# Unequal first tiles (384, 192, 448, then 512 tokens) in a fused sliding-window attention and gated feed-forward kernel

## The chip, the core and the metric

The kernel runs on one core of a Trainium2 chip. TensorE (PE in the profile, PEld for its weight loads) multiplies, VectorE (DVE), ScalarE (ACT) and GpSimd (POOL) do the rest, and the DMA queues of SyncE (SP) and POOL move data between HBM and the on-chip memory SBUF. TensorE writes its sums to PSUM, which has eight banks of 128 partitions x 512 fp32 numbers. The metric is the device time of one execution in microseconds.

## The reference

```
scores = q @ k^T / 8                      # batch 8, heads 8, 576 positions, 64 columns a head
attn   = softmax over the last 64 positions, the own one included
x      = (attn @ v), heads joined         # 4608 tokens x 512
gate   = max(x @ w_gate, 0)               # 512 x 1536
val    = x @ w_val                        # 512 x 1536
out    = (gate * val) @ w_out             # 1536 x 512, result 4608 x 512 in fp32
```

All three weights and q, k, v come in fp32; the kernel computes in fp16 with fp32 sums.

## The kernel before, in words

**Tiles.** The 4608 tokens are taken in tiles: four of 384 tokens (numbers 0 to 3) and six of 512 (4 to 9). For each tile there is an attention part, which makes `xt` (x, transposed, in fp16), a hidden part (gate and val, multiplied into `g_sb`) and an output part (`g_sb` times `wo`).

**Two ways to multiply.** The hidden part of tiles 0 and 1 is done plainly (`first_hidden` for the first four of the 12 blocks of 128 hidden columns, then `hidden`; matmuls at L638, L643 and L605). From tile 2 on, `fast_hidden` (L709) uses seven block products in place of eight: P1 to P7, on sums of quarters of the weights (`us`, `vs`, made by `w_form`, L539) and of x (`xc`, made by `x_form`, L517). The quarters of a weight are columns 0 to 767 against 768 to 1535, so a weight sum needs both halves of a weight. Snapshots of running sums go from PSUM to `pr` (ACT, L728), to another bank (`seed`, ACT, L718), are added by DVE (L745) and multiplied by DVE or POOL (L734). Outputs are plain for tiles 0 and 1 (`output`, L1100) and 2 and 3 (`fast_output`, L842), and by seven products for tiles 4 to 9 (`SevenOut`, `SevenLast`, L922), which need sums of `wo` (`o_form`, L863, on POOL).

**Attention.** The scores of tiles 0 to 3 are made in units of 192 tokens (`u_st`, `u_exp`, `u_mask`, `u_pv`, `u_norm`, `u_turn`), those of the later tiles in quads of four windows of 64 tokens (`q_st`, `q_exp` L441, `q_mask` L446, `values`: `t_pv` L476, `t_recip`, `t_norm` L495, `t_turn` L501). A batch of 576 positions is loaded by POOL's DMA queue (`qk_load`, `v_load`); q and k are then transposed by DVE (L199), and rows of v are copied to a second place (`v_spread`: by SP's DMA at L217 or by an engine's copy at L215).

**Order.** No scheduler runs: the program is issued in an order that a small planner, `Weaver`, sets. PE's work is written down in order and advances a clock; work for other engines is put into a heap with a time (`W.at(T, fn)`) and issued when that clock has passed T, or earlier when something is needed. In the output part of tile 3, three rows of 128 tokens, `values` of tile 4 come ahead of the first two rows and `scores` of tile 5's two quads ahead of the last two; tile 4's own quads were scored in the output part of tile 2. On each engine the instructions then run strictly in the order of issue. PSUM banks are handed out by `one_bank`/`two_banks` in turn for tiles 0 and 1, and by a list of free banks (`bank`) later; a matmul that starts a bank waits until the engine that read its last content is done. `behind_masks`, `behind_quad` put a tiny POOL copy into POOL's queue that waits for a mask on DVE, so that POOL's next long operation starts only after it.

**In time.** PE begins the hidden part of tile 0 at 15.1 us. Weights come in load groups of four blocks (`G3`, `V3`, `O3`), from 7.5 us on. Tiles 0 and 1 with their outputs take until 68.1 us, tile 2 until 92.5 us, tile 3 until 117.3 us, the six tiles of 512 to the end. Within tile 0, PE works on blocks 4 to 7 in banks 0 to 3 (four matmul groups of gate weights, then four of val weights), and then starts blocks 8, 9 and 10 in banks 0, 1 and 2, which DVE's `gate` (L586) has to free; between these, `u_pv(2)` (L347) is done, in banks 4 and 5.

Of the kernel before, what the change touches and what calls it, by code (L numbers as in the profile page):

```python
# [47 lines left out]
def kernel(  # L48
# [24 lines left out]
    NS = 4  # L73
    NL = (NT - NS * TT) // WT
    assert NT == NS * TT + NL * WT and TT % 128 == 0
    starts = [TT * t for t in range(NS)] + [NS * TT + WT * t for t in range(NL)]
    widths = [TT] * NS + [WT] * NL

# [347 lines left out]
    def q_window(qd, i):  # L426
        return NS * TT // 64 + QW * qd + i

    def q_st(qd, banks=None):
# [4 lines left out]
                   for hh in range(2) for i in range(QW)] for g in range(G)])  # L434
        written.update((id(to), 512) for to in d["st"])
        return 0.72

    def q_exp(qd, g, give=True):
        d = quads[qd]
        d["p"][g] = a_p.tile([128, 2 * QW, 64], FP16, name="pw", tag="p")  # L440
        nc.scalar.activation(d["p"][g].rearrange("p n c -> p (n c)"), d["st"][g], ACT.Exp, scale=scale)  # L441
        read(d["st"][g], give)

    def q_mask(qd, g):
        d = quads[qd]
        nc.vector.tensor_tensor(d["p"][g], d["p"][g], mask[:, None, :].to_broadcast([128, 2 * QW, 64]), MUL)  # L446
        d["masked"] = d.get("masked", 0) + 1

    def scores(qd, T, banks=None, give=True):

        W.clock += q_st(qd, banks)
        for g in range(G):
            late = 0.8 if qd > 4 and qd % 2 and g == G - 1 else 0.0
# [3 lines left out]
    def t_pv(t, hh, banks, give):  # L457

        if t not in wides:
            wides[t] = {"pv": {}, "give": give, "x": a_n.tile([128, 2, WS, 2, D // 2], FP16, name="xw", bufs=1),  # L460
# [5 lines left out]
        for qh in range(2):  # L466
            qd = 2 * (t - NS) + qh
            while quads[qd].get("masked", 0) < G:
                W.pop()
            for i in range(QW):  # L470
# [10 lines left out]
    def t_part(d, hh, k):  # L481

        s0, s1 = BS * k, min(BS * k + BS, WS)
        return d["pv"][hh][k][:, 0:(s1 - s0) * VW].rearrange("p (s c) -> p s c", c=VW), s0, s1

    def t_recip(t, hh):
        d = wides[t]
        for k in (2, 0, 1):
# [3 lines left out]
    def t_norm(t, hh, k):  # L492
        d = wides[t]
        pv, s0, s1 = t_part(d, hh, k)
        nc.vector.tensor_tensor(d["x"][:, hh, s0:s1], pv[:, :, 0:D].rearrange("p s (c e) -> p s e c", e=2),  # L495
                                d["r"][:, hh, s0:s1, :, None].to_broadcast([128, s1 - s0, 2, D // 2]), MUL)
        read(d["pv"][hh][k], d["give"])

    def t_turn(t, hh):
        dst = xt_tile(t)[:, 2 * hh:2 * hh + 2].rearrange("p e (s c) -> p s e c", c=32)  # L500
        nc.vector.transpose(dst, wides[t]["x"][:, hh])  # L501
# [9 lines left out]
    def x_form(t, n):  # L511
# [5 lines left out]
        (nc.vector if t <= NS or t - 1 in FAST_OUT else nc.gpsimd).tensor_tensor(xc[:, n], x, y, SUB)  # L517
        if n == 3:
            normed[0] = t

    def values(t, hh, T, banks=None, give=False, turn=2.7):
# [4 lines left out]
        for i, k in enumerate((2, 0, 1)):  # L526
# [5 lines left out]
    def w_form(eng, wt, n, j):  # L532
# [3 lines left out]
        f = slice(256 * j + 128 * HF, 256 * j + 128 * HF + 256)  # L536
        a11, a12, a21, a22 = wt[:, 0:2, c], wt[:, 2:4, c], wt[:, 0:2, f], wt[:, 2:4, f]
# [30 lines left out]
    def hidden(t, spans, f0=0, f1=NF, each=1, halves={}, split=(), banks=None):  # L568

        if t not in gs:  # L570
            gs[t] = g_sb_p.tile([128, NF, WT], FP16, name="g_sb"), {}
        g_sb, done = gs[t]
# [12 lines left out]
        def gate(f, c0, r_sb, h2):  # L585
            nc.vector.tensor_tensor(g_sb[:, f:f + w, c0:c0 + n], part(r_sb), part(h2), MUL)  # L586
            done.update(dict.fromkeys(range(f, f + w), c0 + n))

        for fb in range(f0, f1, each):
            r2s = [f_sb.tile([128, 2, WT], FP32, name="pr", bufs=4) for _ in range(2)]  # L590
            r_sbs = {}
            for i, wt in enumerate((wg, wv)):
                items = [(c0, f) for c0, _ in spans for f in range(fb, fb + each, w)]
                first = halves.get((fb, i), 1)
                for group in [items[:first]] + [[item] for item in items[first:]]:
                    hs = [singles[banks.pop(0)] if banks else one_bank() for _ in group]
                    part_written(hs)
                    for cs in ((0, 1), (2, 3)) if len(group) > 1 else (range(NC),):
                        for (c0, f), h in zip(group, hs):
                            for b in range(w):  # L600
                                W.advance(W.clock)
                                w_need(wt, f + b, cs[-1] // 2)
                                m = n // 2 if i == 0 and f in split else n
# [67 lines left out]
    def fast_hidden(t, seven=None):  # L671

        g_sb, done = gs[t] = g_sb_p.tile([128, NF, WT], FP16, name="g_sb"), {}
# [4 lines left out]
        gh = g_sb[:, :, 0:TW].rearrange("p f (h n) -> p f h n", h=2)  # L678
# [4 lines left out]
        def operands(name, wt, sums, j):  # L683
            c = slice(256 * j, 256 * j + 256)
            f = slice(256 * j + 128 * HF, 256 * j + 128 * HF + 256)
            return {"P1": (wt[:, 0:2, c], b11), "P2": (wt[:, 2:4, c], b21), "P3": (sums[:, 3, :, c], b22),
# [45 lines left out]
        def mult(eng, j, n, h, r, v, to=None):  # L732
            f = 2 * j + HF * n
# [5 lines left out]
        def add(j, name, i, n, delay):  # L739

            def summed():
# [11 lines left out]
                else:  # L753
                    def product_of():
                        late = seven and j == last
                        mult(nc.vector if late else nc.gpsimd, j, n, 1, pr[:, 0], pr[:, 1])
                        if late and n == 1 and t != LAST - 1:
                            nc.gpsimd.tensor_copy(last2[0:1], g_sb[0:1, HF + 2 * j, WT // 2:WT // 2 + 2])
                            g_form(nc.gpsimd, t, 1, j - 1)
                            g_form(nc.gpsimd, t, 2, 0)  # L760
                        if seven and n == 0:
                            for s in range(1 if j == last - 1 and t != LAST - 1 else 2):
                                g_form(nc.vector if late else nc.gpsimd, t, s, j)
                            if late:
                                for jj in (j,) if t + 2 <= LAST else (j, 1) if t == LAST else range(3):
                                    g_form(nc.vector, t, 2, jj)
                                nc.gpsimd.tensor_copy(last2[0:1], g_sb[0:1, HF - 1, 0:2])
# [646 lines left out]
```

## Time and profile before

| what | value |
|---|---|
| median of 3 runs | 300.97 us (300.72 to 301.99) |
| the profiled execution | 300.6 us, of it 298.9 us span |
| granted clock | 0.999 |
| PE busy | 288.8 us, 4657 matmuls recorded |
| DVE, ACT, POOL busy | 251.7, 196.9, 200.8 us |
| from the first full hidden matmuls to tile 4 | 15.6 to 117.3 us |
| tiles 4 to 9 | 117.3 to 298.9 us |

The span is what lies between the first and the last instruction; some 1.7 us of the profiled execution lie around it. A busy PE is not PE at its peak, since matmuls overlap and their ends are modelled: what counts is the distance from one matmul's start to the next one's, which the timeline gives for a run of equal matmuls. A few matmul records are missing, so counts in the views can be a little under those of the program.

### The profile page before, as it was taken

The page shows a single profiled execution, that of the slowest core. Times are in us where ns is not written, and L with a number is a line of the kernel's source. Part 1 is how long each engine was busy: PE and PEld are TensorE (multiplying, and loading weights), DVE is VectorE, ACT ScalarE, POOL GpSimd, SP SyncE. Part 2 cuts the span into 40 slices and gives each one's busy share as a digit, 9 for nine tenths or more (in the row PEclk, how much of TensorE's full clock was granted, in tenths as well). Part 3 has the DMA queues.
Part 4 walks back from the last instruction along what each step waited for, and adds up shares of the span by engine and source line. Part 5 has one row for each costly group of instructions (what it writes and reads, how often), then busy time and mean ns, then how long its engine had stood idle before and what let it go on. Part 6 is the DMA issues. An engine that isn't in the chain of part 4 may idle for free.

```text
span 298.9 us, 11099 instructions
## 1 busy us (share of the span) xinstructions
PE 288.8 (97%) x4657; PEld 239.9 (80%) x4657; DVE 251.7 (84%) x513; ACT 196.9 (66%) x410; POOL 200.8 (67%) x240
## 2 busy tenths in 40 slices
PE   4799999999999999999999999999999999999994
PEld 2486867949958966888888888888888888888894
DVE  5948986998995899779999999989858985896584
ACT  3745236358848847984798579857985798538850
POOL 8768699858967883985958595759375617441750
PEclk9999999999999999999999999999999999999999
DMA  7999999989919636911499239922911210021013
GB/s 215 181 197 201 195 194 185 194 149 191 81 43 201 156 83 129 141 42 36 69 220 119 55 59 219 125 56 58 172 35 36 76 38 0 3 100 45 1 37 105
DMA packets 59506, 33.20 MB, mean 111 GB/s; under 512 B 39552, under 2 KB 53824, under 8 KB 59456
## 3 DMA queue, kind: packets, MB, share of 16 engines
q0 software_dynamic: 46688, 18.29, 52.5%
q1 hardware_dynamic: 12192, 13.75, 15.3%
q8 instruction: 36, 0.59, 0.8%
q10 hardware_dynamic: 576, 0.46, 0.5%
q14 instruction: 14, 0.11, 0.1%
HBM read 37.75 MB, written 9.44 MB: 158 GB/s over the span
## 4 chain that ended last, share of the span: by engine, by line
PE 94%; DVE 3%; DMA 1%; ACT 0%; issue 0%; DVEq 0%
PE bank L709 46%; PE bank L922 18%; PE bank L605 9%; PE bank L842 5%; PE bank L1100 5%; PE bank L276 4%; PE bank L476 3%; PE bank L347 1%; DMA vs<-in_k_dram 1%; PE bank L643 1%; DVE qT L199 1%; DVE kT L199 1%; PE bank L638 0%; PE bank L240 0%; ACT nats L192 0%; DVE pr L1088 0%
## 5 line engine op out<-in xcount | busy, mean ns | idle before, releaser
L734 POOL TENSOR_TENSOR g_sb<-pr 128x512 f16<-128x512 f32 (+1 forms) x36 | 42.7, 1191 | 42.6 <-ACT pr L751 42.5
L745 DVE TENSOR_TENSOR pr<-bank,pr 128x512 f32<-128x512 f32 (+1 forms) x96 | 58.5, 650 | 3.6 <-PE bank L709 1.9
L728 ACT COPY pr<-bank 128x512 f32<-128x512 f32 (+1 forms) x96 | 49.1, 566 | 13.7 <-PE bank L709 13.5
L734 DVE TENSOR_TENSOR g_sb<-r,bank 128x512 f16<-128x512 f32 (+1 forms) x48 | 31.3, 652 | 22.8 <-ACT r L778 22.2
L922 PEld LDWEIGHTS <-g_sb 128*128 128x128 f16 x444 | 41.8, 98 | 5.0
L709 PE MATMUL bank<-xc,us 128*128 128x256 f16 (+2 forms) x292 | 41.3, 265 | 0.0
L709 PE MATMUL bank<-xc,vs 128*128 128x256 f16 (+2 forms) x292 | 41.3, 265 | 0.0
L709 PEld LDWEIGHTS <-vs 128*128 128x128 f16 x388 | 36.6, 98 | 3.4
L709 PEld LDWEIGHTS <-us 128*128 128x128 f16 x388 | 36.6, 98 | 3.2
L205 POOL DMA_DIRECT2D v<-in_v_dram x41 | 34.8, 873 | 2.2 <-DMA nats<-in_q_dram 1.0
L751 ACT ACTIVATE pr<-pr 128x512 f32<-128x512 f32 (+1 forms) x48 | 29.3, 610 | 9.7 <-DVE pr L745 9.7
L778 ACT ACTIVATE r<-bank 128x512 f32<-128x512 f32 (+1 forms) x48 | 27.7, 576 | 4.9 <-PE bank L709 4.0
L709 PEld LDWEIGHTS <-wg 128*128 128x128 f16 x288 | 27.4, 98 | 3.2
L709 PEld LDWEIGHTS <-wv 128*128 128x128 f16 x288 | 27.4, 98 | 2.6
L709 PE MATMUL bank<-xt,wv 128*128 128x256 f16 (+1 forms) x192 | 27.5, 266 | 0.0
L709 PE MATMUL bank<-xt,wg 128*128 128x256 f16 (+1 forms) x192 | 27.5, 266 | 0.0
L872 POOL TENSOR_TENSOR g_sb<-g_sb,xus 128x512 f16<-128x512 f16 x24 | 27.0, 1145 | 0.0
L922 PE MATMUL bank<-wo,g_sb 128*128 128x256 f16 (+1 forms) x222 | 26.6, 270 | 0.0
L441 ACT ACTIVATE pw<-bank 128x512 f16<-128x512 f32 x48 | 25.3, 607 | 1.1 <-PE bank L276 0.7
L922 PE MATMUL bank<-wts,g_sb 128*128 128x256 f16 (+1 forms) x222 | 25.6, 270 | 0.0
L718 ACT COPY bank<-bank 128x512 f32<-128x512 f32 (+1 forms) x48 | 24.5, 552 | 0.0
L310 ACT ACTIVATE p<-bank 128x384 f16<-128x384 f32 (+1 forms) x40 | 14.2, 444 | 10.0 <-PE bank L276 9.9
(120 smaller groups left out, 557.1 us busy)
## 6 DMA issues: line engine op xcount, KB each, us to landing
out_dram<-o_sb SPq DMA_DIRECT2D x30, 256.0 KB, 3.2
nats<-in_k_dram POOLq DMA_DIRECT2D x15, 288.0 KB, 5.5
nats<-in_q_dram POOLq DMA_DIRECT2D x15, 288.0 KB, 8.0
v<-in_v_dram POOLq DMA_DIRECT2D x31, 128.0 KB, 8.0
v<-v SPq DMA_DIRECT2D x27, 66.0 KB, 3.1
v<-v SPq DMA_DIRECT2D x13, 132.0 KB, 2.5
wg<-in_moe_w_gate_dram POOLq DMA_DIRECT2D x6, 256.0 KB, 6.5
wv<-in_moe_w_val_dram POOLq DMA_DIRECT2D x6, 256.0 KB, 8.1
```

The lines of the kernel that those rows point to most:

```text
L205: nc.gpsimd.dma_start(v16s[b % 2][lo:hi, g, :, 0:64], v[b, :, 64 * g - 64 + lo:64 * g - 64 + hi].rearrange("h p d -> p h d"))
L441: nc.scalar.activation(d["p"][g].rearrange("p n c -> p (n c)"), d["st"][g], ACT.Exp, scale=scale)
L605: nc.tensor.matmul(h[:, b * n + lo:b * n + lo + m], wt[:, c, (f + b) * 128:(f + b) * 128 + 128], xt[:, c, c0 + lo:c0 + lo + m], start=(c = ...
L709: nc.tensor.matmul(to[:, HT * m + lo:HT * m + lo + step], w[:, k, 128 * m:128 * m + 128], x[:, k, lo:lo + step], start=(first and m == 0 a ...
L718: nc.scalar.copy(at[j, "B", i][:, 0:TW], at[j, "A", i][:, 0:TW])
L728: nc.scalar.copy(pr[:, i], at[j, "A", i][:, 0:TW])
L734: eng.tensor_tensor(gh[:, f:f + 2, h], pair(r), pair(v), MUL)
L745: nc.vector.tensor_tensor(pr[:, i], to[:, 0:TW], pr[:, i], ADD)
L751: nc.scalar.activation(pr[:, 0], pr[:, 0], ACT.Relu)
L778: nc.scalar.activation(r, to[:, 0:TW], ACT.Relu)
L872: eng.tensor_tensor(to, x, y, op)
L922: nc.tensor.matmul(at[key][:, QN * m * whole:QN * m * whole + n1 - n0], A[:, 128 * m:128 * m + 128], B[:, c, n0:n1], start=(first and m == ...
```

## The change

The tiles become 384, 192, 448 and seven of 512 tokens (numbers 0 to 9 again). Tiles 0 and 1 are plain, so 576 tokens have plain hidden parts instead of 768; tiles 2 to 9 use the seven products in the hidden part. Tile 1's last 64 tokens have their hidden values put in front of tile 2's in `g_sb`, so that outputs are made for 512 tokens (0 and 1 together, minus those 64) and 512 tokens (the 64 and tile 2). The outputs of the first 512 tokens are made in one go, four rows of 128 tokens for each load group of `wo`. Outputs by seven products still begin at tile 4.

The quarters of the weights are now taken within a load group (two blocks of 128 against the next two), so a weight sum needs one load group only. Fourteen of the 24 sums are made by DVE at 16.2, 20.9 and 29.7 us of the planner's clock: four before and eight behind the gates of `first_hidden`, the eight ahead of the masks of unit 2, and two behind unit 2's transposes; ten are POOL's, from 44.7 us on. Before, DVE made eight (at 48.2 and 64.5) and POOL sixteen. Batch 1's tokens all belong to tiles 2 and 3 (quads instead of units), v of that batch is loaded between the load groups of `wo`, and part of it is spread by DVE copies. In the output part of tiles 2 and 3, the scores of the next tile's quads come first and its values one row of output later; tile 5's quads follow, the last after the last row. Some 512-column and 384-column matmuls are issued as two halves (`SPLIT`, `OUT_SPLIT`).

```
-    NS = 4
-    NL = (NT - NS * TT) // WT
-    starts = [TT * t for t in range(NS)] + [NS * TT + WT * t for t in range(NL)]
-    widths = [TT] * NS + [WT] * NL
+    NS = 2
+    NQ = WT - (TT + U) % WT
+    NL = (NT - TT - U - NQ) // WT
+    widths = [TT, U, NQ] + [WT] * NL
+    starts = [sum(widths[:t]) for t in range(len(widths))]
...
+    def q_wins(qd):
+        return range(NQ // 64 - QW if qd == 1 else QW)
...
-            late = 0.8 if qd > 4 and qd % 2 and g == G - 1 else 0.0
+            late = 0.8 if qd > 8 and qd % 2 and g == G - 1 else 0.0
...
+    def behind_x(t):
+        nc.gpsimd.tensor_copy(last[0:1], xc_tile(t)[0:1, 3, 0, 0:2])
...
     def w_form(eng, wt, n, j):
         c = slice(256 * j, 256 * j + 256)
-        f = slice(256 * j + 128 * HF, 256 * j + 128 * HF + 256)
-        a11, a12, a21, a22 = wt[:, 0:2, c], wt[:, 2:4, c], wt[:, 0:2, f], wt[:, 2:4, f]
+        a11, a12, a21, a22 = (wt[:, 2 * k:2 * k + 2, 512 * j + 256 * m:512 * j + 256 * m + 256] for m in range(2) for k in range(2))
...
         def gate(f, c0, r_sb, h2):
-            nc.vector.tensor_tensor(g_sb[:, f:f + w, c0:c0 + n], part(r_sb), part(h2), MUL)
-            done.update(dict.fromkeys(range(f, f + w), c0 + n))
+            if t == 0:
+                nc.vector.tensor_tensor(g_sb[:, f:f + w, c0:c0 + n], part(r_sb), part(h2), MUL)
+                done.update(dict.fromkeys(range(f, f + w), c0 + n))
+                return
+            m = WT - TT
+            nc.vector.tensor_tensor(g_sb[:, f:f + w, TT:WT], part(r_sb)[:, :, 0:m], part(h2)[:, :, 0:m], MUL)
+            nc.vector.tensor_tensor(gs[2][0][:, f:f + w, 0:n - m], part(r_sb)[:, :, m:n], part(h2)[:, :, m:n], MUL)
...
-                                m = n // 2 if i == 0 and f in split else n
+                                m = n // 2 if (i, f) in split else n
...
-    F_LAST = [f for j in range(NF // 4) for f in (2 * j + HF, 2 * j + HF + 1, 2 * j, 2 * j + 1)]
+    F_LAST = [f for j in range(NF // 4) for f in (4 * j + 2, 4 * j + 3, 4 * j, 4 * j + 1)]
...
-        n = DM // 2 if t == 0 and NF - 1 > f >= 9 else DM
+        n = DM // 2 if NF - 1 > f >= OUT_SPLIT else DM
...
+    SPLIT, OUT_SPLIT = [(0, 4 + i) for i in range(8)] + [(1, 4 + i) for i in range(4)], 3
...
-        for n in range(3):
-            w_load(*O3[n], 38.6 + 2.6 * n)
-        for u in (4, 5):
-            v_load(u)
+        w_load(*O3[0], 38.6)
+        v_load(4)
+        v_load(5, ((7, 0, 128),))
+        for n in (1, 2):
+            w_load(*O3[n], 39.6 + 2.6 * n)
+        v_load(5, ((NG - 1, 64, 128),))
...
+        W.at(37.9, lambda: scores(0, 37.9, singles[4:8], False))
+        W.at(41.2, lambda: scores(1, 41.2, singles[4:8], False))
+        W.at(44.6, lambda: behind_quad(1))
+        for hh, T in enumerate((45.0, 45.7)):
+            W.at(T, lambda hh=hh, T=T: values(2, hh, T, singles[4 + 2 * hh:6 + 2 * hh], True, 1.75))
+        for n, T in enumerate((46.8, 49.2, 49.3, 49.4)):
+            W.at(T, lambda n=n: x_form(2, n))
+        W.at(36.4, lambda: v_spread(3, pool))
+        for u in (4, 5):
+            W.at(41.9, lambda u=u: v_spread(u, dve))
+        plan_batch(2, (36.5, 36.6, 38.0, 38.1), (52.9, 53.0, 57.5, 62.0))
+        W.at(50.5, lambda: behind_x(2))
...
-        for T, gap, eng, some in ((41.5, 0.1, nc.gpsimd, sums[0][:4] + sums[1][:3]), (52.8, 0.1, nc.gpsimd, sums[1][3:8]),
-                                  (48.2, 0.6, nc.vector, sums[0][4:8]), (68.1, 0.1, nc.gpsimd, sums[0][8:]),
-                                  (64.5, 0.7, nc.vector, sums[1][8:])):
+        for T, gap, eng, some in ((16.2, 0.0, nc.vector, sums[0][:4]), (20.9, 0.0, nc.vector, sums[1][:4] + sums[0][4:8]),
+                                  (29.7, 0.0, nc.vector, sums[1][4:6]),
+                                  (44.7, 0.1, nc.gpsimd, sums[1][6:8] + sums[0][8:10]), (50.6, 0.1, nc.gpsimd, sums[0][10:12] + sums[1][8:])):
...
-        hidden(0, ((0, TT),), 4, NF, 4, split=(4, 5), halves={(8, 0): 3, (8, 1): 2})
+        hidden(0, ((0, TT),), 4, NF, 4, split=SPLIT, halves={(8, 0): 3, (8, 1): 2})
         hidden(1, ((0, U),), each=4, banks=[0, 1, 4, 5, 2, 3, 0, 1, 2, 3, 0, 1])
         taken["one"] += 2
-        output(0, (0, 1, 2), (0, 4, 8, NF))
-        ready(1)
-        hidden(1, ((U, TT),), each=4)
-        output(1)
+        output(0, (0, 1, 2, 3), (0, 4, 8, NF))
...
-            between = [[] for _ in range(widths[t] // 128)]
-            if t + 1 < NS:
-                for u in (2 * t + 2, 2 * t + 3):
-                    between[0].append(lambda u=u: unit_values(u, W.clock))
-            elif t + 1 <= LAST:
-                for hh in range(2):
-                    between[hh].append(lambda hh=hh: values(t + 1, hh, W.clock))
-            if t + 2 <= LAST:
-                for qh in range(2):
-                    between[qh - 2].append(lambda qh=qh: scores(2 * (t + 2 - NS) + qh, W.clock))
+            qd = 2 * (t + 1 - NS)
+            score = lambda n: lambda: scores(qd + n, W.clock)
+            value = lambda hh: lambda: values(t + 1, hh, W.clock)
+            between = [[score(0)], [score(1)], [value(0), value(1)], []]
+            if t == 3:
+                between[3].append(score(2))
             fast_output(t, between)
+            if t == 3:
+                score(3)()
```

## The prediction

> **What bounds the kernel now.** I read the profile's page first, then the chain that ended last, then the timeline of each engine around the places that the change touches.
>
> ```profile
> PE 94%; DVE 3%; DMA 1%; ACT 0%; issue 0%; DVEq 0%
> ```
>
> TensorE carries 94% of the chain; the rest is the start, ahead of 15.6 us, and the tail. So a shorter matmul stream shortens the run, and everything else counts only where PE has to wait for it. From the chain, in order of time (start, us, what):
>
> ```profile
> 27.42 10.60 PE bank L605 x100
> ...
> 68.11 14.07 PE bank L709 x168
> 82.18 0.96 PE bank L347 x86
> ...
> 92.49 14.12 PE bank L709 x168
> ...
> 147.62 16.59 PE bank L709 x152
> 164.22 1.31 PE bank L922 x12
> ```
>
> 152 matmuls of 256 columns take 16.60 us, 109.2 ns each. The two 384-wide tiles need 14.07 and 14.12 us for 168 of 192 columns. What 192 and 384 columns cost undisturbed is in PE's timeline:
>
> ```profile
> 26.02 0.92 PE L605 MATMUL bank<-xt,wg 128*128 128x384 f16 x4
> 26.86 0.56 PE L347 MATMUL bank<-v,p 128*32 128x65 f16 x48
> 27.36 2.13 PE L605 MATMUL bank<-xt,wg 128*128 128x384 f16 x12
> 29.32 2.76 PE L605 MATMUL bank<-xt,wv 128*128 128x384 f16 x16
> 31.92 1.48 PE L605 MATMUL bank<-xt,wg 128*128 128x192 f16 x16
> 33.24 1.48 PE L605 MATMUL bank<-xt,wv 128*128 128x192 f16 x16
> ```
>
> From start to start, 16 of 384 columns take 2.60 us (162.5 ns each), 16 of 192 take 1.32 us (82.5 ns). The first line is the place to watch: its four should end at 26.67 and PV follows at 26.86, so PE already waits 0.2 us for DVE to free a bank.
>
> **Part 1, the matmul stream.** In program order the change takes 352 matmuls of 192 columns, 40 of 384 and 26 of 512 out and puts 168 of 224 and 220 of 256 in; scores, PV and the seven-product outputs keep their counts. 512 columns cost 225 ns (12 of L842 from 83.08 to 85.78 us); 224 columns are between 82.5 and 109.2, by their middle 95.9 ns. Sum: -352 x 82.5 = -29.04 us, -40 x 162.5 = -6.50, -26 x 225 = -5.85, +168 x 95.9 = +16.11, +220 x 109.2 = +24.02: **-1.26 us**. That is 2304 columns fewer, an eighth of 192 tokens' hidden part, plus what halving the long matmuls gives.
>
> The Trainium skill, page "TensorE: Matmul & The Clock Gate", section "Back-to-back issue gap" (its phase diagram stands just above), puts 512 columns at some 216 ns and 256 at 109 ns. By that, halving a 512 gains nothing, and the sum would be -1.02 us; the rows here say 225 against 2 x 109.2, and the measurement decides.
>
> **Part 2, stalls that go.** 168 x 82.5 is 13.86 us; the two 384-wide tiles lose 0.21 and 0.27 us to ACT's and DVE's work on their products. The 512-wide tiles lose nothing (109.2 each, all through). In their place come a tile of 448, between the two (I leave it 0.1), and one of 512: **-0.38 us**, bounds 0 and -0.48.
>
> **Part 3, eight weight sums on DVE ahead of unit 2's masks.** DVE and POOL before:
>
> ```profile
> 20.41 0.56 DVE L654 TENSOR_TENSOR g_sb<-pr,bank 128x384 f16<-128x384 f32 x1
> 23.40 1.42 DVE L317 TENSOR_TENSOR p<-p,mask 128x384 f16<-128x384 f16 x3 [2.44 <-ACT p L310]
> ...
> 24.75 0.54 DVE L586 TENSOR_TENSOR g_sb<-pr,bank 128x384 f16<-128x384 f32 x1
> 25.21 0.72 DVE L317 TENSOR_TENSOR p<-p,mask 128x384 f16<-128x384 f16 x1
> 25.86 1.47 DVE L586 TENSOR_TENSOR g_sb<-pr,bank 128x384 f16<-128x384 f32 x3
> ```
> ```profile
> 23.83 1.89 POOL L215 COPY v<-v 64x512 f16<-64x512 f16 x2 [2.77 <-DMA v<-in_v_dram]
> ```
>
> DVE is free from 20.9 to 23.4 us, 2.5 us. The eight sums take more: L539 rows of DVE last 0.42 us, follow each other at 0.34, and at 0.45 where one needs the last: 8 sums, 3.2 us, done at 24.1. Their weights are there (the last of them lands at 20.1 us). The masks thus start 0.7 us late, and inside POOL's two copies of v. That matters, as the masks' group shows:
>
> ```profile
> L317 DVE TENSOR_TENSOR p<-p,mask x24: 336/352/1317, 23.4 to 68.3; 128x384 f16<-128x384 f16 x24
> ```
>
> The 1.32 us is the mask at 39.6, which began just behind a POOL sum of 1.15 us and ended after it; the one at 25.21 waited for a copy. DVE's fp16 work in SBUF stands still while POOL runs a tensor operation; gates, which read PSUM, do not (24.75: 0.54). Walked: the first mask waits for copy one (24.6), the second for copy two (25.75), third done at 26.2; gate of bank 0 at 26.7, fourth mask, gate of bank 1 at 27.4. PE wants bank 0 at 26.02 and bank 1 0.33 later: it starts at 26.75, waits again until 27.45, and is at its next matmuls behind PV at 28.29, where it was at 27.36: **+0.93 us**. Bounds: +0.07 if the second mask gets in ahead of copy two (gate of bank 1 at 26.55), +1.6 if a sum is caught by a copy too. I take the walk. Four sums at 16.2 lie in DVE's idle time up to 18.5 and cost nothing; without that, 0.42 each.
>
> The backlog runs on: DVE's queue from 28.35 (reciprocals to transposes 2.2, two sums 0.8, four gates at 0.47, four transposes of q and k at 1.09, two split gates at 0.52) ends near 38.6, and PE wants that bank for quad 0's scores at 38.8. **+0.1**, bounds 0 and +0.6.
>
> **Part 4, transfers and queues.** Two v loads (near 1 us each in the queue) go ahead of the second and third group of `wo`, which then land near 43.8 and 46.4 instead of 41.8 and 44.4. PE uses them at some 45.7 and 50.3: nothing, else 1 us for each us over 1.9. POOL's next issues wait for these landings, so its queue is free at 47.3. Its ten sums of 1.15 us then run, with a wait of 2.5 us for `behind_x`, to 61.5. The tile-2 stage starts near 53.9 and uses the last of them 17 steps of 0.77 us later, at 66: 4 us of cover. DVE's copies of v (1.4 us in all) replace SP transfers and lie ahead of PV at 47.
>
> **Part 5, values one output row after their scores.** Before, PV of tile 4 came a whole hidden part after its masks. Now scores, one row of 12 matmuls (2.70 us), PV: four exps at 0.49, the first 0.2 behind the scores, end at +2.2, the last mask (0.42) at +2.7. No cover is left, and two transposes of 1.09 us are in DVE's queue there. **+0.25 us** in tile 3's output, bounds 0 and +1.5 (one POOL product of 1.28 in the way).
>
> **Part 6, scores behind the last row of tile 3.** Now tile 4 follows on them at once.
>
> ```profile
> 117.31 0.58 ACT L847 COPY o_sb<-bank 128x512 f32<-128x512 f32 x1 [0.62 <-PE bank L842]
> 117.80 1.07 ACT L718 COPY bank<-bank 128x512 f32<-128x512 f32 x2
> ```
>
> In ACT's queue exps and seeds now alternate: exp, seed, exp. With S the start of tile 4's P1: first exp at S+0.2, seed at S+0.69, second exp from S+1.17 to S+1.77. P5's second half starts the bank of that second exp, and PE wants it after P1 (0.87) and 8 short matmuls (0.45), at S+1.32. **+0.45 us**, bounds 0 and +0.6.
>
> **The sum.** -1.26 - 0.38 + 0.93 + 0.1 + 0.25 + 0.45 = **+0.09 us**, on 300.6 of the profiled execution, which is 0.37 under the median of its runs: 301.1 on the median. From 117.3 us on, 181.6 us of matmuls keep their order.
>
> **The rivals.**
> *The masks get through (299.5).* No wait in parts 3 and 5: -1.26 - 0.48 + 0.07 + 0 + 0 + 0.2 = -1.47. For it: DVE is only 0.7 us late and 25.21 shows that a mask can also go between copies; against it, the wait at 26.67 is there already.
> *The lock between DVE and POOL decides (302.9, slower).* Tile 3's output is the place: eight masks stand in front of PV, and POOL works off products of 1.28 us and `wo` sums of 1.15 there. Each mask that starts behind one loses up to its length, as at 39.6; the one collision in my sum costs 0.25 since half a us is spare, each further one its full 1.2. Two more (at both tiles' values) are +2.4, less 0.6 of what part 3 may save: +1.8. It decides from the second further collision on. The Trainium skill, page "SBUF — State Buffer", section "Who interferes with whom", states that a DVE operation with two SBUF inputs and a GpSimd operation that reads SBUF block each other fully; by that rule, the trace agrees (1.32 against 0.35 us).
> *The sums come late (304).* POOL's last ones miss tile 2's third step by more than 4 us, for a queue held by landings. Against it: slack of 4 us. Then tile 2 does not gain what part 1 says, +3.
>
> **How the numbers follow.** 0.5% is 1.5 us, about what a measurement of this kernel can tell from no change. Forecast 0.58 (0.52 of it within 0.5%, 0.02 faster, 0.04 slower), masks through 0.20 (half beyond 0.5%), the lock 0.17 (0.14 slower), late sums 0.05: faster 0.12, same 0.65, slower 0.23. Low ends together: -1.26 - 0.48 + 0.07 = -1.67, 299.3; high: -1.26 + 1.6 + 0.6 + 1.5 + 0.6, less 0.3 for not all at once, = +2.7. I cut both a little: 299.4 to 303.2.
>
> **What would show it.** Right: 152 matmuls of tile 3 at 109 ns, a hole of some 1.1 us in PE between 26 and 28 us with DVE gates as releaser, one of near 0.4 us right behind tile 4's first eight matmuls with ACT as releaser, and tile 4 starting near 116.9 us (117.3 less 0.36). Wrong: no hole near 27 us (then -1), long masks (over 0.5 us) near 105 to 111 us, a PE wait for `us` or `vs` between 62 and 66 us, or any hole in the six last tiles, which I take as unchanged.

## The result and the profile after

The changed kernel takes 301.95 us (median; 301.05 to 302.81), the kernel before 301.01 us (300.49 to 301.99) beside it: ratio 1.0031, 95% interval 1.0021 to 1.0041. Forecast were 301.1 us and "within 0.5%"; that holds, with the median 0.85 us above the forecast. The profiled execution took 301.29 us, of it 299.6 us span (before 298.9). The sum of the prediction is made against profiles, and there it is +0.7 where +0.09 was forecast.

The chain that ended last of the changed kernel, by engine:

```profile
PE 89%; DVE 6%; DMA 1%; issue 1%; ACT 1%; DVEq 0%
```

TensorE still bounds the kernel, but 1% is new: "issue", time in which an engine waited for nothing that the profile shows. Where it is, PE's timeline of the changed kernel says (start, us, line, operation, count; in brackets the idle time before and its releaser):

```profile
26.07 0.49 PE L634 MATMUL bank<-xt,wg 128*128 128x192 f16 x4
26.98 0.49 PE L634 MATMUL bank<-xt,wg 128*128 128x192 f16 x4 [0.42 <-DVE g_sb L609]
27.40 0.56 PE L348 MATMUL bank<-v,p 128*32 128x65 f16 x48
27.89 2.15 PE L634 MATMUL bank<-xt,wg 128*128 128x192 f16 x24
...
117.20 0.61 PE L740 MATMUL bank<-xc,us 128*128 128x128 f16 x8
118.15 0.61 PE L740 MATMUL bank<-xc,vs 128*128 128x128 f16 x8 [0.35 <-ACT pw L450]
...
136.50 1.47 PE L956 MATMUL bank<-wo,g_sb 128*128 128x256 f16 x12
137.90 1.32 PE L493 MATMUL bank<-v,pw 128*32 128x65 f16 x127
139.48 0.19 PE L493 MATMUL bank<-v,pw 128*32 128x65 f16 x1 [0.26 <-issue]
...
198.99 1.34 PE L493 MATMUL bank<-v,pw 128*32 128x65 f16 x128
200.27 0.94 PE L956 MATMUL bank<-wts,xus 128*128 128x256 f16 x7
201.78 0.71 PE L956 MATMUL bank<-wts,xus 128*128 128x256 f16 x5 [0.58 <-issue]
```

The first two groups are the holes that the prediction named, behind DVE's gates and behind ACT's exps. Counted from start to start, beyond the usual distance, they cost 0.58 and 0.51 us. The last two (0.44 and 0.74 us) and a third of 0.28 us at 52.3 us were not foreseen: the trace shows nothing that PE waited for, and it stopped in the middle of a run of equal matmuls. The kernel before has no such hole at these places. Its PE timeline where the last one would be:

```profile
198.85 1.34 PE L476 MATMUL bank<-v,pw 128*32 128x65 f16 x128
200.12 1.48 PE L922 MATMUL bank<-wts,xus 128*128 128x256 f16 x12
```

What ends the hole at 118.15 us is ACT's queue, in which exps (L450) and seeds (L749) alternate as forecast:

```profile
116.43 0.60 ACT L450 ACTIVATE pw<-bank 128x512 f16<-128x512 f32 x1
117.02 0.57 ACT L749 COPY bank<-bank 128x512 f32<-128x512 f32 x1
117.50 0.60 ACT L450 ACTIVATE pw<-bank 128x512 f16<-128x512 f32 x1
117.99 0.61 ACT L749 COPY bank<-bank 128x512 f32<-128x512 f32 x1
```

**Where the time went.** Start to start on PE, before against after. Up to tile 4's first matmul (117.11 against 116.31 us) the change gains 0.80 us; forecast was 0.36. Then tile 4 loses the 0.51, and of the tiles behind it only the spans with holes differ: 30.35 to 31.29 us from tile 4 to 5 (0.51 and 0.44), 30.33 to 30.34, 30.34 to 31.07 (0.74), 30.24 to 30.32 (0.08, one more small hole at 232.4 us). From the last matmul to the end it is 0.30 us shorter; why stays open. -0.80 + 0.51 + 0.44 + 0.01 + 0.73 + 0.08 - 0.30 = +0.67.

### The profile page after: what moved, and what is told of

Same layout as the page of the kernel before. It is cut to its first block, busy times and chain, and to the rows that moved or that the text cites. A ratio compares the mean times of both kernels' runs of the same rounds, so it can differ in the third digit from the quotient of the medians.

```text
span 299.6 us, 10994 instructions
## 1 busy us (share of the span) xinstructions
PE 288.8 (96%) x4627; PEld 242.2 (81%) x4627; DVE 256.7 (86%) x513; ACT 198.7 (66%) x400; POOL 193.9 (65%) x223
## 3 DMA queue, kind: packets, MB, share of 16 engines
q1 hardware_dynamic: 11808, 13.41, 15.1%
## 4 chain that ended last, share of the span: by engine, by line
PE 89%; DVE 6%; DMA 1%; issue 1%; ACT 1%; DVEq 0%
PE bank L740 48%; PE bank L956 19%; PE bank L874 5%; PE bank L634 4%; PE bank L1135 4%; PE bank L493 3%; PE bank L277 3%; DVE kT L200 2%; PE bank L672 1%; DMA vs<-in_k_dram 1%; DVE qT L200 1%; DVE pw L459 1%; PE bank L348 1%; DVE p L318 1%; ACT pw L450 1%
## 5 line engine op out<-in xcount | busy, mean ns | idle before, releaser
L765 POOL TENSOR_TENSOR g_sb<-pr 128x512 f16<-128x512 f32 (+1 forms) x36 | 45.2, 1256 | 41.8 <-ACT pr L782 41.5
L776 DVE TENSOR_TENSOR pr<-bank,pr 128x512 f32<-128x512 f32 (+1 forms) x96 | 60.9, 674 | 3.3 <-PE bank L740 1.9
L759 ACT COPY pr<-bank 128x512 f32<-128x512 f32 (+1 forms) x96 | 51.0, 587 | 14.0 <-PE bank L740 13.9
L765 DVE TENSOR_TENSOR g_sb<-r,bank 128x512 f16<-128x512 f32 (+1 forms) x48 | 32.5, 677 | 22.7 <-ACT r L809 21.0
L740 PE MATMUL bank<-xc,vs 128*128 128x256 f16 (+2 forms) x292 | 42.7, 269 | 0.3 <-ACT pw L450 0.3
L740 PE MATMUL bank<-xc,us 128*128 128x256 f16 (+2 forms) x292 | 42.7, 269 | 0.0
L740 PEld LDWEIGHTS <-vs 128*128 128x128 f16 x388 | 37.6, 98 | 4.3 <-issue 0.5
L450 ACT ACTIVATE pw<-bank 128x512 f16<-128x512 f32 x60 | 32.1, 606 | 2.1 <-PE bank L277 1.7
L749 ACT COPY bank<-bank 128x512 f32<-128x512 f32 (+1 forms) x48 | 25.6, 573 | 0.0
L459 DVE TENSOR_TENSOR pw<-pw,mask 128x512 f16<-128x512 f16 x60 | 23.5, 437 | 2.1 <-ACT pw L450 1.7
```

Source lines behind the costliest of these rows:

```text
L740: nc.tensor.matmul(to[:, HT * m + lo:HT * m + lo + step], w[:, k, 128 * m:128 * m + 128], x[:, k, lo:lo + step], start=(first and m == 0 a ...
L749: nc.scalar.copy(at[j, "B", i][:, 0:TW], at[j, "A", i][:, 0:TW])
L759: nc.scalar.copy(pr[:, i], at[j, "A", i][:, 0:TW])
L765: eng.tensor_tensor(gh[:, f:f + 2, h], pair(r), pair(v), MUL)
L776: nc.vector.tensor_tensor(pr[:, i], to[:, 0:TW], pr[:, i], ADD)
```

## The experiments

Two theories of the holes without a releaser were tested. *Instruction blocks*: PE's instructions come by DMA (queue 8 of the profile: 36 packets, 0.59 MB, so 16 KB each); 9254 weight loads and matmuls over 36 packets are 257 a packet; if a block is 256 instructions, it holds 128 pairs of a weight load and a matmul. A *limit* is the place where one block ends and the next begins. The three holes stand behind pairs 863, 2270 and 3294: 1407 = 11 x 128 - 1 and 1024 = 8 x 128 apart. PV (attention weights times v) of a 512-wide tile is 128 short pairs in 1.35 us, so it can use up a whole block before the next one has come. *Order of work*: some wait of the new order that the trace does not show. The new order itself (parts 3 and 6 of the prediction) was tested beside it.

### 1 and 2: more pairs near 14 us (e1, e2)

In PE's idle time near 14 us, 40 small matmuls of zeros are added (e2: the kernel before, 40 there and 66 in place of a filler):

```
+        for i in range(40):
+            g = 32 * (i % 4)
+            nc.tensor.matmul(to[g:g + 32, 0:16], zero[:, 0:32], zero[:, 0:16], start=False, stop=False, ...)
         heat(1, units[1]["st"][3])
```

> The changed kernel with 40 small matmuls of zeros (32 weights, 16 columns) in TensorE's idle time near 14 us; nothing else moves. Theory of the instruction blocks: TensorE's instructions come in blocks of 16 KB, 256 instructions or 128 pairs of weight load and matmul; the three holes that no engine released (52.3, 139.0 and 200.9 us; 0.28 + 0.44 + 0.74 = 1.46 us) lie 11 and 8 such blocks apart, each where a whole block was a burst of short PV matmuls (128 pairs in 1.4 us), so that the next block was not there yet. 80 more instructions ahead of it move the block limits away from the bursts: no hole without a releaser over 0.15 us, and the time falls by 1.2 to 1.8 us, to 0.994 to 0.998 of the kernel before. Theory of a new wait in the order of work (a semaphore or a transfer that the trace does not show): the holes stay at the same matmuls, and the time stays within 0.3 us of the changed kernel's, 1.002 to 1.004 of before.

> The kernel before with 104 such matmuls net ahead of 14 us (66 in place of one long filler matmul, 40 in the idle time). Theory of the instruction blocks: the limits now fall on the PV bursts of tiles 5 to 8, where the changed kernel has them; by the durations of its own blocks of 128 pairs against 2.45 us (fetch of a block until its first instruction runs), holes without a releaser of 0.5 to 1.1 us at two to four of 139, 170, 200 and 231 us, together 1.5 to 3.3 us, and a time of 1.004 to 1.012 of the kernel before. Theory of a new wait in the order of work: this kernel keeps its order, so no such hole, and 1.000 to 1.002 for the small matmuls themselves.

Measured: 308.41 us (1.0221, interval 1.0176 to 1.0267) and 308.68 us (1.0234, 1.0196 to 1.0271). Both times are missed by far: e1 was to become faster by the first theory and became slower, and e2 became slower by much more than forecast. The holes at 139 and 201 us are gone from e1, and the kernel before, its order untouched, now has them (0.20, 0.25 and 0.80 us, behind or just after the PV of three tiles, and 1.82 us in a burst at 61.4, besides 3.9 us in a PV between the added matmuls). But the added matmuls are themselves a burst of short pairs, at a time when the DMA engines are at least 90% busy (10 to 18 us). PE's timeline of e1:

```profile
14.06 0.35 PE L244 MATMUL bank<-wts 128*32 128x16 f16 x17
17.28 0.32 PE L244 MATMUL bank<-wts 128*32 128x16 f16 x23 [2.86 <-issue]
...
18.42 2.74 PE L673 MATMUL bank<-xt,wg 128*128 128x384 f16 x8
```

PE stops inside the dummies, behind pair 223 = 95 + 128, for 3.0 us. Its block is on the way from 14.90 to 15.79 us, and PE goes on 1.5 us after that. The last line shows a second price: eight matmuls of 384 columns take 320 ns each in place of 162, half speed. The trace's granted clock is 0.5 there (18.4 to 21.8 us), and again from 56.0 to 59.4 us. The shift also brought limits into bursts at 53 and 121 us (2.2 and 1.1 us) and one into long matmuls at 33 us (0.6 us), where the block's packet started 3.7 us behind the limit before it.

### 3 and 4: parts 3 and 6 on top of e1

```
-(20.9, 0.0, nc.vector, sums[1][:4] + sums[0][4:8]),
+(20.9, 0.0, nc.vector, sums[1][:4]), (44.9, 0.0, nc.vector, sums[0][4:8]),      # e3
-                score(3)()
+                scores(qd + 3, W.clock - 0.75)                                   # e4
```

> e1_after_pad40 with four of the eight weight sums of 20.9 us (those of us, second group) on DVE at 44.9 us, behind quad 1's masks. If part 3 of the prediction is right that the eight sums make the masks and gates late: PE's wait at 26.3 us (0.58 us excess) falls to at most 0.2, and the time by 0.4 us against e1; the four sums at 45.7 to 47.4 us are hidden, since DVE is idle there for 1.5 us. If the copies of v on POOL and not the sums hold the masks: the wait stays over 0.4 us, and the time within 0.15 us of e1.

> e1_after_pad40 with the exps of tile 5's second quad planned 0.75 us sooner, so that ACT's queue at the start of tile 4 is copy, exp, exp, seed, exp, seed, exp in place of copy, exp, seed, exp, seed, exp, exp. If part 6 is right that PE waits for the second exp behind a seed: PE's wait at 117.6 us (0.51 us) falls to under 0.1, and the time by 0.4 us against e1. If the seeds are as urgent as the exps: a wait of 0.2 us or more comes back within the next 2 us at the product that follows the seed (P2 or P6), and the time falls by 0.25 or less.

Measured: 308.96 us (1.0245, 1.0209 to 1.0281) and 308.10 us (1.0208, 1.0163 to 1.0254). With holes of 2 to 3 us that come and go the times tell nothing, and e3's wait at DVE's gates was covered by PE's late start. e4's trace does tell. PE's timeline at the start of its tile 4:

```profile
123.97 0.61 PE L746 MATMUL bank<-xc,vs 128*128 128x128 f16 x8
124.42 0.60 PE L746 MATMUL bank<-xc,us 128*128 128x256 f16 x4
125.39 0.60 PE L746 MATMUL bank<-xc,vs 128*128 128x256 f16 x4 [0.37 <-ACT bank L755]
```

P5 no longer waits for the second exp, but P6 waits for the second seed, 0.54 us from start to start: the wait has only moved on. The order that helps must put both exps and both seeds first.

### 5 and 6: the limits moved without a burst (e5, e6)

```
-    HALVED = ((4, 0, 'P5'),)
+    HALVED = ((4, 0, 'P5'),) + tuple((4, 1, p) for p in ('P1', 'P6', 'P2', 'P7', 'P5'))   # e5; e6: 13 products
```

> The changed kernel with five more products of tile 4 in halves of 128 columns (the second step's P1, P6, P2, P7, P5): 40 more pairs of weight load and matmul between 122 and 131 us, no new burst, and nothing earlier moves. Price by 128 columns at 56 ns: 40 x (2 x 56 - 109.2) ns = 0.11 us. Theory of the instruction blocks: from tile 5 on the block limits lie 40 pairs sooner, some 38 matmuls ahead of the PV bursts, as in the kernel before; the holes at 139.0 and 200.9 us go (0.44 + 0.74 us in the profiled execution; by the medians, which lie 0.66 us further apart than the profiles, up to 1.8), the hole at 52.3 us (0.28) stays, and the time is 0.995 to 0.999 of the kernel before. Theory of a wait in the order of work: holes and time as in the changed kernel, 1.003.

> The kernel before with 13 more products of tile 4 in halves of 128 columns: 104 more pairs between 122 and 143 us, price 0.29 us, order of work unchanged. Theory of the instruction blocks: a limit now falls within 10 pairs of the start of the PV bursts of tiles 5 to 8, so a block lasts some 1.6 to 2 us there, and holes without a releaser of 0.2 to 1 us come at two to four of them (139, 170, 200, 231 us), 0.6 to 2.5 us together: 1.003 to 1.009 of the kernel before. Theory of a wait in the changed order of work: no holes, 1.001.

Measured: e5 300.67 us (0.9988, interval 0.9970 to 1.0006), e6 303.32 us (1.0077, 1.0049 to 1.0104). PE's timeline of e5 at the places of the two late holes:

```profile
138.49 1.34 PE L493 MATMUL bank<-v,pw 128*32 128x65 f16 x128
139.77 1.05 PE L956 MATMUL bank<-wts,xus 128*128 128x256 f16 x8
...
199.16 1.34 PE L493 MATMUL bank<-v,pw 128*32 128x65 f16 x128
200.43 1.48 PE L956 MATMUL bank<-wts,xus 128*128 128x256 f16 x12
```

and of e6, the kernel before with more pairs:

```profile
230.88 1.25 PE L476 MATMUL bank<-v,pw 128*32 128x65 f16 x128
232.06 0.72 PE L922 MATMUL bank<-wts,xus 128*128 128x256 f16 x5
233.42 0.92 PE L922 MATMUL bank<-wts,xus 128*128 128x256 f16 x7 [0.64 <-issue]
```

Forty matmuls in halves, which cost 0.11 us by the estimate ahead of the run, make the changed kernel 1.28 us faster by the medians; the intervals against the kernel before do not overlap. The hole at 52.3 us, ahead of the edit, stays (0.26). The other way round, the kernel before with its order unchanged loses 2.25 us, of which halving explains 0.29. Its profile shows one such hole (0.80 us) and a start 1.5 us late, with a granted clock of 0.5 from 11.2 to 14.7 us, so how the rest splits up in the other executions stays open. The clock does not explain the loss: the four executions with a mean clock of 0.998 or more took 302.48 to 303.59 us, and the fastest of them is 1.96 us above the fastest of before. The theory of a wait in the order of work falls.

Over all kernels of this study, 26 holes of 0.2 us and more without a releaser stand behind pair 94 or 95 of a group of 128, counted from PE's first matmul. The only others lie around the long filler matmuls ahead of 14 us, and one of 0.21 us at 58 to 59 us in e1 and e3 is no stop but a matmul at the clock of 0.5.

### 7 and 8: the sums later, and the limit at 52.3 us (e7, e8)

e7 is e5 with e3's edit. e8 adds:

```
-    SPLIT, OUT_SPLIT = [(0, 4 + i) for i in range(8)] + [(1, 4 + i) for i in range(4)], 3
+    SPLIT, OUT_SPLIT = [(0, 4 + i) for i in range(8)], 3
-    HALVED = ... ('P1', 'P6', 'P2', 'P7', 'P5'))
+    HALVED = ... ('P1', 'P6', 'P2', 'P7', 'P5', 'P4', 'P3'))
```

> e5_after_late40 with four of the eight weight sums of 20.9 us on DVE at 44.9 us, behind quad 1's masks. If the eight sums make the masks and gates late (part 3): PE's wait at 26.3 us (0.58 us excess in the changed kernel) falls to at most 0.2 and the time by 0.4 us against e5; the four sums run in DVE's idle time at 45.7 to 47.3 us. If POOL's copies of v hold the masks and not the sums: the wait stays over 0.4 us and the time within 0.15 us of e5.

> e7 with the wv products of the second group of tile 0 not in halves (16 pairs fewer near 24 us, price at 162.5 against 2 x 82.5 ns a gain of 0.04 us) and seven in place of five products of tile 4 in halves (56 pairs more, 0.05 us), so that the limits from tile 5 on are those of e5. Theory of the instruction blocks: the limit at 52.3 us moves 16 pairs on, the block with tile 2's PV bursts (5.1 us long) gets 1.7 us longer, and the hole of 0.28 us goes: 0.3 us less than e7, no hole without a releaser over 0.15 us. If it does not go, something else than the blocks makes that one.

Measured: e7 299.92 us (0.9961, interval 0.9945 to 0.9978), 0.75 us less than e5 in the same series; e8 299.85 us (0.9954, 0.9937 to 0.9971). The eight sums thus do cost time, more than the 0.4 expected: PE's two waits at the gates were 1.05 us in e5's profile, and one of 0.33 us is left in e7's (0.41 in e8's). So neither theory of e7 was whole. In e8 no hole without a releaser over 0.15 us is left behind 15 us, the one at 52.3 us included; its time is only 0.07 us under e7's, less than the two can be told apart by.

The profile of e5 explains the size. DVE's timeline of the changed kernel:

```profile
24.05 1.30 DVE L318 TENSOR_TENSOR p<-p,mask 128x384 f16<-128x384 f16 x3
25.28 0.54 DVE L609 TENSOR_TENSOR g_sb<-pr,bank 128x384 f16<-128x384 f32 x1
```

and of e5, the same program up to tile 4:

```profile
24.11 2.14 DVE L318 TENSOR_TENSOR p<-p,mask 128x384 f16<-128x384 f16 x3
26.18 0.54 DVE L609 TENSOR_TENSOR g_sb<-pr,bank 128x384 f16<-128x384 f32 x1
```

Three masks take 1.30 us in one execution and 2.14 in the other, and the gate behind them, which frees PE's next bank, starts 0.9 us later. In the first POOL's copies of v ran from 24.41 us, in the second, where v landed sooner, from 23.82, over all three masks. PE is at its next matmuls behind PV at 27.89 us in the one and at 28.41 in the other; the prediction's walk said 28.29.

### 9: the copies of v on ACT (e9)

```
-        v_spread(2, pool)
+        nc.gpsimd.tensor_copy(last[0:1], v16s[0][64:65, NG - 1, 0, 0:2])
+        W.at(24.6, lambda: v_spread(2, act))
```

> e8 with unit 2's two copies of v on ACT, behind its four exps, in place of POOL (one tiny POOL copy still waits for the landing of v, so POOL's loads issue when they did). If POOL's copies are what makes unit 2's masks long: each mask takes 0.35 us (three took 2.24 us in e8), PE's wait near 26.5 us (0.41 us) falls to at most 0.1, and the time by 0.3 to 0.4 us against e8. If the masks are held by something else: they stay long and the time stays within 0.15 us.

Measured: 299.21 us (0.9942, interval 0.9929 to 0.9955). DVE's timeline of e8:

```profile
23.46 2.24 DVE L318 TENSOR_TENSOR p<-p,mask 128x384 f16<-128x384 f16 x3 [0.86 <-ACT p L311]
```

and of e9:

```profile
23.30 1.12 DVE L318 TENSOR_TENSOR p<-p,mask 128x384 f16<-128x384 f16 x3 [0.86 <-ACT p L311]
24.34 0.55 DVE L609 TENSOR_TENSOR g_sb<-pr,bank 128x384 f16<-128x384 f32 x1
24.83 0.36 DVE L318 TENSOR_TENSOR p<-p,mask 128x384 f16<-128x384 f16 x1
```

With the copies off POOL the masks take half the time (0.36 us the fourth), the gate runs 1.3 us sooner than in e8, and PE's wait is gone. POOL's copies are shown to be what stretches the masks. The times of e8 and e9 come from two series; by the ratios the gain is 0.36 us, as expected, though the intervals overlap.

### 10: two exps, two seeds (e10)

e8 with the exps of tile 5's second quad at -0.75 us and the last two of them 0.6 us later:

```
-                score(3)()
+                scores(qd + 3, W.clock - 0.75, gap=0.6)
```

> e8 with ACT's queue at the start of tile 4 as copy, exp, exp, seed, seed, exp, exp. e4 moved the wait from the second exp to the second seed (0.54 us at P6 in place of 0.51 at P5), so both orders lack one place. If the chain is only these four: no wait over 0.1 us in tile 4's first 4 us and 0.4 to 0.5 us less than e8. If the last two exps are urgent as well (their banks, or POOL's queue behind quad 7): a wait of 0.3 us or more by 122 us, and less than 0.2 us gained.

Measured: 299.46 us (0.9946, interval 0.9933 to 0.9958). ACT's timeline of e10 at the start of tile 4:

```profile
116.00 1.08 ACT L450 ACTIVATE pw<-bank 128x512 f16<-128x512 f32 x2
116.97 1.09 ACT L750 COPY bank<-bank 128x512 f32<-128x512 f32 x2
117.96 1.11 ACT L450 ACTIVATE pw<-bank 128x512 f16<-128x512 f32 x2
118.93 1.11 ACT L760 COPY pr<-bank 128x512 f32<-128x512 f32 x2
```

P5 and P6 run without a wait. The wait of 0.51 us is gone and one of 0.18 us comes in its place, at 119.6 us behind the snapshots of the last line: 0.33 gained on PE, between the two expectations. By the ratios the time is 0.24 us under e8's, with intervals that overlap.

### 11 and 12: output rows in halves, and all together (e11, e12)

```
-                nc.tensor.matmul(op, g_sb[:, f, ...], wo[:, f], start=(i == 0), stop=(i == NF - 1))
+                n = DM // 2 if (t, sub) in ROWS else DM
+                for lo in range(0, DM, n):
+                    nc.tensor.matmul(op[:, lo:lo + n], g_sb[:, f, ...], wo[:, f, lo:lo + n], start=(i == 0 and lo == 0), ...)
+    ROWS = ((2, 0), (2, 2), (2, 3), (3, 0), (3, 1), (3, 3))      # and HALVED as in the changed kernel
```

> e8 with six of the eight output rows of tiles 2 and 3 in halves of 256 columns (72 more pairs) and without the seven halved products of tile 4 (56 pairs fewer), so that the limits from tile 5 on lie 56 pairs ahead of the changed kernel's. By the rows of the profile (512 columns 225 ns, 256 columns 109.2): a row of 12 falls from 2.70 to 2.62 us, 72 x 6.6 = 0.48 us, and 56 x 2.8 ns = 0.16 us from tile 4: 0.6 us less than e8. By the Trainium skill, page TensorE: Matmul & The Clock Gate, section Back-to-back issue gap (some 216 ns for 512 columns, 109 for 256): a row does not change, and 0.16 us in all. No hole without a releaser over 0.15 us by either.

> e9, e10 and e11 together: the sum of what each gains on e8 by the readings above, 0.35 + 0.45 + 0.6 = 1.4 us, 298.4 to 298.9, or 0.990 to 0.993 of the kernel before. If the gains overlap (a wait that only moves on), the sum is missed by over 0.4 us.

Measured: e11 302.16 us (1.0038, interval 1.0018 to 1.0057), e12 301.33 us (1.0015, 1.0000 to 1.0030): slower than e8, by 2.5 and 1.8 us as the ratios have it. e11 expected no hole and e12 the sum of the gains, and both were wrong. PE's timeline of e11:

```profile
73.63 2.77 PE L876 MATMUL bank<-wo,g_sb 128*128 128x512 f16 x12
76.32 1.32 PE L493 MATMUL bank<-v,pw 128*32 128x65 f16 x128
77.57 5.41 PE L876 MATMUL bank<-wo,g_sb 128*128 128x256 f16 x48
82.82 0.60 PE L740 MATMUL bank<-xt,wg 128*128 128x256 f16 x4
...
112.09 0.49 PE L277 MATMUL bank<-qT,kT 32*128 32x64 f16 x39
114.91 0.37 PE L277 MATMUL bank<-qT,kT 32*128 32x64 f16 x25 [2.33 <-issue]
```

The added pairs brought a limit (pair 1886 = 94 + 14 x 128) into the scores at 112.4 us. The block before it lasted 3.8 us (from 108.56 us), and an earlier one of 3.7 us (from 73.06 us) passed without a hole, its packet starting at once; here the packet began only 3.9 us after the limit, at 112.44 us, while the DMA engines were 90% busy with batches of k, q and v and an output. The granted clock was 0.5 from 115.9 to 119.4 us as well in this execution, so its profile is longer than the hole alone makes it. e12, at a clock of 1.0 throughout, has the same hole (2.22 us) and a second one (0.73). Without these 2.95 us its profile (span 300.1 us) would stand at 297.1, so the other gains add up there, but that is worked out and not shown.

The rows also settle the price of 512 columns. Two rows in halves take 82.82 - 77.57 = 5.25 us, 109.4 ns a matmul. A whole row takes 2.69 us up to the next burst, but of that 0.1 us is the change from full matmuls to PV's: 12 matmuls of 256 columns in the fence of PE above take 1.40 us from 136.50 us, 0.09 more than 12 x 109.2. That leaves 216 ns, and a list of all starts says the same (median 216 ns in the kernels before and after).

## Why the prediction was right in number, and where it failed

**Right for part of its reasons.** The forecast of no change that counts holds, and three of its waits are where it put them (parts 3, 5 and 6). But in its profile the changed kernel lost 1.54 us (0.28 + 0.44 + 0.74 + 0.08) by a mechanism that the prediction does not have. Gains that it left out or losses that it took too large paid for 1.05 of that: the tail 0.30, a burst 0.20, part 3 some 0.45, the backlog 0.10. That the sum came out within 0.6 us is luck.

**The step that failed**, though the number held, is the sentence "From 117.3 us on, 181.6 us of matmuls keep their order", with nothing in the sum for them. They do keep it, and e5 shows that the order costs nothing. What changed is how many instructions stand ahead: the limits of PE's instruction blocks moved by 30 pairs (4624 matmuls in the program for 4654) onto the starts of the PV bursts. A tile of 512 is 508 pairs, four short of four blocks, so a limit that meets the PV of one tile meets that of the next three as well: here it falls 1 pair ahead of the first PV and 3, 7 and 11 pairs inside the others, where in the kernel before it lay 31, 27, 23 and 19 pairs ahead. The prediction had listed "any hole in the six last tiles" as what would prove it wrong, and that is how it was found.

By its steps:

- *Part 1*, -1.26: the term of 512 columns was mis-sized. 225 ns was a row divided by 12 with the change to the next burst in it; start to start it is 216. The sum is -1.02. The Trainium skill (page "TensorE: Matmul & The Clock Gate", section "Back-to-back issue gap") has that number, for what it calls the isolated gap, and the trace agrees with it, 216 ns; the 131 ns that the section gives for a sustained stream is not what these streams show. The prediction weighed the 216 and chose wrongly. 224 columns, taken as 95.9 ns, measure 95.8.
- *Part 2*, -0.38: right. The two tiles' 0.48 us are gone, the 448-wide one loses 0.07.
- *Part 3*, +0.93: right in mechanism, and its size changes with the landing of v. Of the 0.2 us that it read as a wait at 26.67 us before, 0.1 was a wait and 0.09 the change from full matmuls to PV's. The part is +0.53 in the profile of the changed kernel, 0.5 more in that of e5. e7 and e9 take the sums and the copies away one after the other, and the wait goes with them. The backlog at quad 0's scores (+0.1) did not come.
- *Part 4*, 0: right. POOL's last sum ends at 61.3 us, against 61.5 forecast, and PE waits for none. The stage of tile 2 starts at 53.8 us, the hole of 0.28 us ahead of it included.
- *Part 5*, +0.25: right, 0.24 us at 108.5 us behind DVE's masks.
- *Part 6*, +0.45: right, 0.51 us, ACT as releaser. e4 and e10 show that exps and seeds compete for ACT.
- *Left out*: one burst fewer ahead of tile 4 (14 for 15). Each costs some 0.2 us at its two edges, so -0.20.

Up to tile 4 that is -1.02 - 0.41 + 0.48 (0.58 less a wait of 0.10 that was there before) + 0.24 - 0.20 + 0.28 = -0.63; what the rest to -0.80 is stays open.

**The rivals.** *The masks get through* came half true in one execution. *The lock between DVE and POOL at tile 3's output* did not decide: one mask of 0.69 us begins at 103.0 us inside a POOL product, the others average 0.35 to 0.55, so there is one collision, where it needed two more. That such a lock exists e9 shows again. *The sums come late* did not happen.

**What beats both kernels.** e7 to e10 do, e9 by most: 299.21 us, ratio 0.9942 (0.9929 to 0.9955). e9 and e10 together, without the rows, were not run.

## What to carry to other kernels

When a change alters how many instructions an engine runs, look for holes without a releaser behind equal distances of instructions, above all in bursts of short ones; a few harmless instructions more or fewer ahead of them test it, as long as these are no burst themselves. Take a matmul's price from start to start within a run of equal ones, not from a row that ends in another kind of work. When a wait has two causes in a row, removing the first shows only a part, and a wait behind a full queue moves to the next in line unless all that are urgent are put first.

## What the runs showed of the hardware

**PE's instruction blocks.** The DMA view of the changed kernel from 198 to 204 us, in 40 slices of 0.15 us:

```profile
DMA  0000000500000000009999930000000050000000
GB/s 0 0 0 0 0 0 0 109 0 0 0 0 0 0 0 0 0 0 300 335 314 328 321 123 14 27 20 21 0 0 0 0 109 0 0 0 0 0 0 0
...
q8 instruction: 2, 0.03, 2.8%
```

The lone entries near 199.1 and 202.9 us are two blocks of 16 KB. The first begins at 199.17 us, just behind the limit that PE crossed at 199.04 us, and is there at 200.56; PE, at the next limit since 201.04, goes on at 201.78, 1.22 us behind the packet's end. At 139 us that distance is 1.22 as well, in the burst of e1 1.5. The packets thus fit a block that is asked for at one limit and needed at the next: if the 128 pairs between last less than the way of the block (from the limit to PE's going on 1.8 us at 139 us and 2.7 us here, 6.4 at the hole of e11, with busy DMA engines), PE stops for the rest. Behind long matmuls the packet can start before the limit's matmul runs, by 1.7 us at 275.75 us, and then the hole gets smaller or does not come. The kernel before has one block as short, 1.3 us from 109.87 us, whose packet started 1.3 us ahead, and no hole. This fits holes at some tiles only. That the median of the changed kernel is 0.66 us above its profiled execution may have the same cause, but the other executions have no trace.

The Trainium skill, page "Runtime: NRT & Kernel Launch", section "Instruction fetch mechanics", states blocks of 16 KiB or 256 instructions that the sequencer fetches by itself, at a cost "mostly hidden". The trace agrees on the block (36 packets of 16 KB); the cost is hidden with 128 pairs in 14 us, and not always with 128 pairs in 1.35 us.

**After some holes of 2 to 4 us the granted clock was 0.5.** In e1 it was so for 3.4 us from 18.4 us, 1.1 us behind the end of a hole of 3.0 us, and matmuls of 384 columns took 320 ns, twice their 162; the same came behind holes of 2.2 us in e1 and 2.5 us in e11. In e4, with holes of 2.9, 2.3 and 2.0 us, and in e12, with 2.2 us, the clock stayed at 1.0. So a long stop can cost more than its own length, and the runs do not show when it does.

**Bursts of small matmuls** cost 0.09 to 0.12 us at either edge: 30 such edges, 3.2 us, between 15.1 us and tile 4 in the kernel before.
